# Both expert matmuls by Strassen's seven products

## The chip, the cores and the metric

The kernel runs on one core of a Trainium2 chip. A core has a matmul engine (PE), three engines for elementwise work (DVE, ACT, POOL), a queue for transfers (SP) and 16 DMA engines between DRAM and its own memory (SBUF; matmuls write to a second memory, PSUM, of eight banks). The metric is the device time of one execution in microseconds (us); lower is better. The kernel before took 2241.37 us in the median of three runs, 2239.83 to 2242.37.

## The reference, cut to what matters

Two layers. The first is attention with decay: for each of 4 sequences and 8 heads a 64 x 64 state is decayed by gamma and a product k v is added at each of 768 positions, and q reads it. The second takes the 3072 x 512 result as x:

```
P = exp(x @ w_gate - max); 8 times: rows, then columns of P are normalized
out = 0
for e in range(8):                          # experts
    h = max(x @ w1[e], 0)                   # 3072 x 512 times 512 x 1024
    out += P[:, e:e+1] * (h @ w2[e])        # 3072 x 1024 times 1024 x 512
```

Every token goes through all eight experts.

## The kernel before

**Precision.** The two expert matmuls run in a reduced format of fp32 that PE takes at full rate. To keep accuracy each operand is split into a high part (a copy, rounded) and a low part (the operand minus its high part), and each product is three matmuls: high x high, low x high, high x low. ACT or POOL makes high parts (`hi_act`, L72, or a cast, L112), DVE or POOL the low ones (`lo`, L75).

**Attention.** 24 chunks of 128 positions (6 chunks of each of 4 sequences). `split_qk` splits q and k, `scores` (L226) multiplies them into `ps_s`, DVE masks the result into `ta` (L229), `attend` (L257, L262) reads the state and adds the chunk's own part, `state` (L238, L244) updates the state. Beside it the kernel already runs the first expert group in units of 256 tokens, and the gate logits.

**Experts.** The hidden dimension of all experts, 8 x 1024, is cut into 16 groups of four tiles of 128. For a group g and a block i of 512 tokens, `b_mm1` makes one hidden tile in `hps2` by 12 matmuls of 512 columns (`mm1`, L121 to L123), `h_split` (L126 on ACT, L127 on DVE) makes the high and low half of its relu, and one tile later `b_mm2` multiplies it with w2 into four banks `ops2` (`mm2`, L132 to L134). After four tiles DVE adds the four banks, times the gate value, to the accumulators `acc` in SBUF (L460 for the first group, L462 then), and the last group stores them (L465). Accumulators of all 3072 tokens stay in SBUF. `x_split` splits the next block's x while this one is multiplied (L72, L75), and POOL splits the weights of the next group (`conv_w`). The 18 steps of the gate normalization are strewn between the first tiles.

Everything stands in the order in which it is written (`manual_schedule`): each engine runs its instructions in that order, and waits by semaphores.

## Time and profile before

| | |
|---|---|
| median of three runs | 2241.37 us |
| the profiled execution's span, first to last instruction | 2238.8 us |
| PE matmul busy | 2219.1 us, 99% |
| PE weight loads busy | 1856.5 us, 83% |
| DVE, ACT, POOL busy | 892.5, 523.2, 349.4 us |
| DMA | 87.46 MB, mean 39 GB/s |
| matmul and weight-load instructions | 10639 each |

Times are of one execution, taken by the hardware profiler. A group's row reads: line, engine, operation, output <- inputs, shapes, count | busy us, mean ns of one | idle time of the engine ahead of it, and what ended it. In rows ordered by time the first number is the start in us from the span's start and the second the length. Matmuls overlap their successors, so one that lasts 0.39 us does not occupy PE for so long; the interval between starts does. The granted clock is the share of full speed that the throttle gives PE.

### The profile page before, as it was taken

To read this page: it belongs to the slowest core of one execution; us is meant where nothing else is said; L and a number is where in the kernel's file an instruction comes from. 1 tells how busy PE (TensorE), PEld (TensorE's weight loads), DVE (VectorE), ACT (ScalarE), POOL (GpSimd) and SP (SyncE) were. 2 spreads that over 40 slices of the span, in tenths; PEclk is the share of its full clock that TensorE was granted. 3 is DMA by queue.
4 is the path that set the end of the run, shared out by engine and by line. 5 is a ranking of instruction groups with operands and counts; after the bars stand their busy time and mean duration, and the time that the engine had idled before them with its cause. 6 is when DMAs were issued, how large, how long until landed. Compare 5 with 4: busy or idle time off the path is not lost.

```text
span 2238.8 us, 25404 instructions
## 1 busy us (share of the span) xinstructions
PE 2219.1 (99%) x10639; PEld 1856.5 (83%) x10639; DVE 892.5 (40%) x1403; ACT 523.2 (23%) x949; POOL 349.4 (16%) x329
## 2 busy tenths in 40 slices
PE   7999999999999999999999999999999999999999
PEld 6999888888888888888888888888888888888887
DVE  5666455333433333343333334333333433333342
ACT  4333321332212122121222212122221212222121
POOL 5554200202020020202002020200202020020200
PEclk9999999999999999999999999999999999999999
DMA  6454350101010010101001010100101010010011
GB/s 206 132 169 128 125 172 5 33 1 38 1 33 6 6 34 1 38 1 33 5 5 34 1 38 1 34 5 5 33 1 38 1 34 5 6 33 1 10 57 57
DMA packets 91027, 87.46 MB, mean 39 GB/s; under 512 B 5792, under 2 KB 66336, under 8 KB 90912
## 3 DMA queue, kind: packets, MB, share of 16 engines
q1 hardware_dynamic: 90624, 84.78, 12.1%
q8 instruction: 84, 1.38, 0.3%
q0 software_dynamic: 288, 1.05, 0.2%
q14 instruction: 31, 0.25, 0.0%
HBM read 69.03 MB, written 16.78 MB: 38 GB/s over the span
## 4 chain that ended last, share of the span: by engine, by line
PE 98%; DVE 1%; SPq 0%; ACT 0%; DMA 0%; issue 0%; ACTq 0%
PE hps L121 16%; PE ops L133 16%; PE ops L132 16%; PE ops L134 16%; PE hps L123 15%; PE hps L122 15%; PE ps_s L226 1%; PE ps_x L262 1%; PE ps_t L238 1%; PE ps_x L257 1%; DVE QL L75 1%; DMA raw<-qT 0%; SPq L176 0%; PE ps_g L291 0%; PE ps_g L290 0%
## 5 line engine op out<-in xcount | busy, mean ns | idle before, releaser
L127 DVE SCALAR_TENSOR_TENSOR hl<-hps,hh 128x512 fp32r<-128x512 f32 x360 | 249.0, 692 | 1218.3 <-ACT hh L126 1218.3
L126 ACT ACTIVATE hh<-hps 128x512 fp32r<-128x512 f32 x360 | 215.6, 599 | 1540.8 <-PE hps L123 1535.4
L123 PE MATMUL hps<-xl,w1h 128*128 128x512 f32 x1440 | 560.6, 389 | 0.9 <-DVE xl L75 0.9
L121 PE MATMUL hps<-xh,w1h 128*128 128x512 f32 x1440 | 561.4, 390 | 0.0
L133 PE MATMUL ops<-w2l,hh 128*128 128x512 f32 x1440 | 560.3, 389 | 0.0
L122 PE MATMUL hps<-xh,w1l 128*128 128x512 f32 x1440 | 560.3, 389 | 0.0
L134 PE MATMUL ops<-w2h,hl 128*128 128x512 f32 x1440 | 560.2, 389 | 0.0
L132 PE MATMUL ops<-w2h,hh 128*128 128x512 f32 x1440 | 560.2, 389 | 0.0
L123 PEld LDWEIGHTS hps<-xl,w1h 128*128 128x128 f32 x1440 | 270.2, 188 | 57.8 <-DVE xl L75 1.4
L121 PEld LDWEIGHTS hps<-xh,w1h 128*128 128x128 f32 x1440 | 270.6, 188 | 56.2
L133 PEld LDWEIGHTS ops<-w2l,hh 128*128 128x128 f32 x1440 | 270.4, 188 | 56.4
L134 PEld LDWEIGHTS ops<-w2h,hl 128*128 128x128 f32 x1440 | 270.4, 188 | 56.0
L132 PEld LDWEIGHTS ops<-w2h,hh 128*128 128x128 f32 x1440 | 270.0, 188 | 55.9
L122 PEld LDWEIGHTS hps<-xh,w1l 128*128 128x128 f32 x1440 | 270.2, 188 | 55.6
L112 POOL CAST w1h<-r 128x512 fp32r<-128x512 f32 x55 | 33.6, 611 | 1450.4 <-PE hps L123 1450.4
L75 DVE TENSOR_TENSOR xl<-x,xh 128x512 fp32r<-128x512 f32 x360 | 229.7, 701 | 0.0
L462 DVE SCALAR_TENSOR_TENSOR acc<-ops,Pm,acc 128x512 f32<-128x512 f32 x336 | 228.4, 743 | 2.1 <-PE ops L134 2.1
L72 ACT ACTIVATE xh<-x 128x512 fp32r<-128x512 f32 x360 | 196.6, 622 | 0.0
L75 POOL TENSOR_TENSOR w1l<-r,w1h 128x512 fp32r<-128x512 f32 x63 | 82.3, 1307 | 43.7 <-ACT w1h L72 36.8
L75 POOL TENSOR_TENSOR w2l<-r,w2h 128x512 fp32r<-128x512 f32 x63 | 86.5, 1373 | 4.4
L75 DVE TENSOR_TENSOR QL<-raw,QH 64x512 fp32r<-64x512 f32 x46 | 61.4, 1334 | 14.6 <-ACT QH L72 13.9
L112 POOL CAST w2h<-r 128x512 fp32r<-128x512 f32 x55 | 36.8, 670 | 141.7 <-PE ops L134 141.7
(101 smaller groups left out, 1163.4 us busy)
## 6 DMA issues: line engine op xcount, KB each, us to landing
r<-w SPq DMA_DIRECT2D x128, 256.0 KB, 2.7
raw<-kT SPq DMA_DIRECT2D x24, 256.0 KB, 4.1
raw<-qT SPq DMA_DIRECT2D x24, 256.0 KB, 3.6
raw<-vn SPq DMA_DIRECT2D x24, 256.0 KB, 5.2
spill<-y SPq DMA_DIRECT2D x24, 256.0 KB, 2.0
acc<-spill SPq DMA_DIRECT2D x24, 256.0 KB, 6.4
out<-acc SPq DMA_DIRECT2D x24, 256.0 KB, 2.1
raw<-kn SPq DMA_DIRECT2D x20, 256.0 KB, 5.2
```

What stands on the lines that cost most here:

```text
L72: act.activation(o, i, AF.Copy)
L75: eng.tensor_tensor(o, full, rd(h), ALU.subtract)
L112: engs[0].tensor_copy(h, r)
L121: pe.matmul(hps[:, :n], w[0][:, k, :], xh[:, k, :], start=(k == 0), stop=False)
L122: pe.matmul(hps[:, :n], w[1][:, k, :], xh[:, k, :], start=False, stop=False)
L123: pe.matmul(hps[:, :n], w[0][:, k, :], xl[:, k, :], start=False, stop=(k == KD - 1))
L126: act.activation(hh, hps[:, :n], AF.Relu)
L127: dve.scalar_tensor_tensor(hl, hps[:, :n], 0.0, rd(hh), ALU.max, ALU.subtract)
L132: pe.matmul(ops[t], hh[:, s], w[2], start=(f == 0), stop=False)
L133: pe.matmul(ops[t], hh[:, s], w[3], start=False, stop=False)
L134: pe.matmul(ops[t], hl[:, s], w[2], start=False, stop=(f == FG - 1))
L462: dve.scalar_tensor_tensor(acc[m], o, Pm[:, m, e:e + 1], acc[m], ALU.mult, ALU.add)
```

## The change

x, w1, h and w2 are cut into 2 x 2 blocks of 256 x 256 (a stretch of 512 hidden units, a chunk of 4 x 128 tokens), and each 2 x 2 block product is formed by seven products of sums and differences of blocks (Winograd's form of Strassen's algorithm, M1 to M7) in place of eight. Each of the seven is still three high/low matmuls over two halves of the contraction and two of the output: 12 matmuls of 256 columns.

The work now stands in two stages. In the first, each of 96 units (16 stretches of hidden units x 6 chunks, `a_step`) multiplies sums of x with sums of w1. PE accumulates in four banks; ACT and DVE combine the seven products (`a_post`), take the relu, and form the four blocks of h and the four sums of them that the second stage needs, seven slices of 128 x 512 in all, that go to DRAM (`hd`). In the second stage a block is one expert and one chunk: two stretches (`jl`) of seven products, 14 steps. SP loads a slice of h for each step 14 steps ahead (`h_load`), ACT and DVE make its high and low part three steps ahead (`h_conv`), and PE multiplies it with sums of w2 (`b_mm`), both stretches into the same seven banks. In the second stretch `b_post` combines the products, scales the result with the gate values (L744, four copies on ACT), and the sum goes to DRAM: plainly for the first expert, by an adding transfer that POOL issues for the other seven. The accumulators in SBUF are gone.

Sums of w1 and w2 are formed and split by POOL (high parts by ACT), those of x by DVE or DVE and POOL, a task at a time between PE's steps (`conv_tasks`, `run`). Beside attention only the stretch 0 of the hidden units runs now. The gate logits are made with plain fp32 matmuls of 8 columns, and the normalization's 18 steps stand between units 2 to 19 of the first stage.

```diff
-UNIT = 256
-NU = N // UNIT
-BLK = 512
-NBLK = N // BLK
+BLK = B * C
 NTILE = N // P
-FG = 4
-NG = E * F // (FG * P)
+HB = BLK // 2
+NJP = E * F // 512
...
+ORD_U = [M1, M5, M2, M6, M3, M7, M4]
+ORD_W1 = [M1, M2, M5, M6, M3, M7, M4]
+ORD_B = [M1, M2, M6, M7, M5, M3, M4]
...
-    def mm1(hps, w, xh, xl, n):
-        for k in range(KD):
-            pe.matmul(hps[:, :n], w[0][:, k, :], xh[:, k, :], start=(k == 0), stop=False)
-            pe.matmul(hps[:, :n], w[1][:, k, :], xh[:, k, :], start=False, stop=False)
-            pe.matmul(hps[:, :n], w[0][:, k, :], xl[:, k, :], start=False, stop=(k == KD - 1))
-
-    def h_split(hps, hh, hl, n):
-        act.activation(hh, hps[:, :n], AF.Relu)
-        dve.scalar_tensor_tensor(hl, hps[:, :n], 0.0, rd(hh), ALU.max, ALU.subtract)
-
-    def mm2(ops, w, hh, hl, f, nt):
-        for t in range(nt):
-            s = slice(t * P, (t + 1) * P)
-            pe.matmul(ops[t], hh[:, s], w[2], start=(f == 0), stop=False)
-            pe.matmul(ops[t], hh[:, s], w[3], start=False, stop=False)
-            pe.matmul(ops[t], hl[:, s], w[2], start=False, stop=(f == FG - 1))
-
...
+    NSA, NSB = 16, 17
+    SLA = cst.tile([P, NSA, 2, 2, HB], F32R, name="SLA")
+    RAW = [cst.tile([P, 4, 512], F32, name=f"RAW{i}") for i in range(3)]
+    SC = cst.tile([P, 4, 512], F32, name="SC")
+    OUTS = cst.tile([P, 8, 512], F32, name="OUTS")
+    TMP = cst.tile([P, 6, 512], F32, name="TMP")
+
+    xd = [drp.tile([P, 4, 512], F32, name=f"xd{i}") for i in range(CPB)]
+    hd = [[drp.tile([P, 7, 512], F32, name=f"hd{j}_{i}") for i in range(CPB)] for j in range(NJP)]
+
...
+    def sums_left(b, s):
+        a11, a12, a21, a22 = b
+        s1, s2, s3, s4 = s
+        return ([(s1, a21, a22, ALU.add), (s2, s1, a11, ALU.subtract),
+                 (s3, a11, a21, ALU.subtract), (s4, a12, s2, ALU.subtract)],
+                [a11, a12, s4, a22, s1, s2, s3], {M5: [0], M6: [0, 1], M7: [2], M3: [0, 1, 3]})
+
+    def sums_right(b, t, neg3):
+        b11, b12, b21, b22 = b
+        t1, t2, t3, t4 = t
+        x, y = (b12, b22) if neg3 else (b22, b12)
+        return ([(t1, b12, b11, ALU.subtract), (t2, b22, t1, ALU.subtract),
+                 (t3, x, y, ALU.subtract), (t4, b21, t2, ALU.subtract)],
+                [b11, b21, b22, t4, t1, t2, t3], {M5: [0], M6: [0, 1], M7: [2], M4: [0, 1, 3]})
+
...
+    def conv_tasks(sums, slots, order, eng_add, eng_lo, done=None):
+        adds, src, need = sums
+        engs = eng_lo if isinstance(eng_lo, list) else [eng_lo] * 7
+        tasks, made = [], set()
+
+        def add(a):
+            eng_add.tensor_tensor(a[0], a[1], a[2], a[3])
+
+        def one(i, e):
+            t = slot(slots[i])
+            hi_act(t[:, 0], src[i])
+            lo(e, t[:, 1], src[i], t[:, 0])
+
+        for k, i in enumerate(order):
+            for a in need.get(i, ()):
+                if a not in made:
+                    made.add(a)
+                    tasks.append((k, lambda a=adds[a]: add(a)))
+            tasks.append((k, lambda i=i, e=engs[k]: one(i, e)))
...
+    def a_mm(u, i):
+        bank = {M1: "A", M6: "A", M7: "A", M4: "A", M2: "B", M5: "C", M3: "C"}[i]
+        new = i in (M1, M2, M5)
+        if new:
+            u.t[bank] = psA[bank]()
+        ps = u.t[bank]
+        w, x = slot(u.w[i]), slot(u.x[i])
+        for j in range(2):
+            for k in range(2):
+                for n, (a, b) in enumerate(((0, 0), (1, 0), (0, 1))):
+                    pe.matmul(ps[:, j, :], w[:, a, k, j * P:(j + 1) * P], x[:, b, k, :],
+                              start=new and j == 0 and k == 0 and n == 0,
+                              stop=j == 1 and k == 1 and n == 2, **kw)
+
...
+    def a_post(u, i):
+        t = u.t
+        if i == M1:
+            t["s1"] = TMP[:, 0, :]
+            act.activation(t["s1"], flat(t["A"]), AF.Copy)
+        elif i == M5:
+            t["s5"] = TMP[:, 1, :]
+            act.activation(t["s5"], flat(t["C"]), AF.Copy)
+        elif i == M2:
+            o = a_out(u, "A11")
+            dve.tensor_tensor(o, flat(t["B"]), t["s1"], ALU.add)
+            act.activation(o, o, AF.Relu)
+            a_store(u, "A11", M1)
+        elif i == M6:
+            t["u2"] = TMP[:, 2, :]
+            act.activation(t["u2"], flat(t["A"]), AF.Copy)
+        elif i == M3:
+            t["c12"] = TMP[:, 3, :]
+            dve.tensor_tensor(t["c12"], flat(t["C"]), t["u2"], ALU.add)
+            o = a_out(u, "S3")
+            dve.scalar_tensor_tensor(o, t["c12"], 0.0, t["A11"], ALU.max, ALU.subtract)
+            a_store(u, "S3", M7)
+        elif i == M7:
+            o = a_out(u, "A22")
+            dve.tensor_tensor(o, flat(t["A"]), t["s5"], ALU.add)
+            act.activation(o, o, AF.Relu)
+            a_store(u, "A22", M4)
+            s1 = a_out(u, "S1")
+            dve.scalar_tensor_tensor(s1, t["c12"], 0.0, o, ALU.max, ALU.add)
+            a_store(u, "S1", M5)
+            s2 = a_out(u, "S2")
+            dve.tensor_tensor(s2, s1, t["A11"], ALU.subtract)
+            a_store(u, "S2", M6)
+        elif i == M4:
+            o = a_out(u, "A12")
+            act.activation(o, flat(t["A"]), AF.Relu)
+            a_store(u, "A12", M2)
+            s4 = a_out(u, "S4")
+            dve.tensor_tensor(s4, o, t["S2"], ALU.subtract)
+            a_store(u, "S4", M3)
+
...
+        sweep = [[5, 4, 3], [0, 1, 2]]
+        units = [(0, 0, 5)] + [(s, jp, c) for s in range(2) for jp in range(1, NJP) for c in sweep[s]]
...
+            seq = [(u, M6), (v, M1), (u, M3), (u, M7), (v, M2), (u, M4), (v, M5)]
+            for m, (w, i) in enumerate(seq):
+                if w is not None:
+                    a_step(w, i)
+                if n > 0 or m > 0:
+                    run(bg, 2)
+                if m % 2 == 0:
+                    run(wq, 1)
+                if job == NJP - 1 and row < 2 and m == 5:
+                    bg += x_conv(sweep[1][row])
+            if 2 <= n < 2 + len(sink):
+                sink[n - 2]()
+            if row == 2:
+                run(wq, 12)
...
+        HR = XS[0] + XS[2]
+        corder = [5, 4, 3, 0, 1, 2]
+        steps = [(e, c, jl, i) for e in range(E) for c in corder for jl in range(2) for i in ORD_B]
...
+        def w2_conv(e, jl):
+            r = raw_at.pop(("w2", e, jl))
+            sl = {i: w2_slot(e, 7 * jl + k) for k, i in enumerate(ORD_B)}
+            t = conv_tasks(sums_right(blocks_w2(r), scratch(SC), True), sl, ORD_B, pool, pool, lambda: raw_done(r))
+            last = NW2 - 14
+            return [(SPE * e + (14 - SPE if k + 7 * jl < last else k + 7 * jl - last - 14), f) for k, f in t]
+
+        def h_load(s):
+            if s < len(steps):
+                e, c, jl, i = steps[s]
+                sp.dma_start(rd(slot(HR[s % NH])[:, 1]).rearrange("p j t -> p (j t)"), hd[2 * e + jl][c][:, i, :])
+
+        def h_conv(s):
+            if s < len(steps):
+                t = slot(HR[s % NH])
+                act.activation(t[:, 0], rd(t[:, 1]), AF.Copy)
+                lo(dve, t[:, 1], rd(t[:, 1]), t[:, 0])
...
+            ps = cur[i]
+            h = slot(HR[s % NH])
+            w = slot(w2_slot(e, 7 * jl + ORD_B.index(i)))
+            for j in range(2):
+                for t in range(2):
+                    for n, (a, b) in enumerate(((0, 0), (0, 1), (1, 0))):
+                        pe.matmul(ps[:, t, :], h[:, a, j, t * P:(t + 1) * P], w[:, b, j, :],
+                                  start=jl == 0 and j == 0 and t == 0 and n == 0,
+                                  stop=jl == 1 and j == 1 and n == 2, **kw)
...
+            if i == M2:
+                dve.tensor_tensor(cc[:, 0, :, 0, :], cur3, h3(m1s), ALU.add)
+            elif i == M6:
+                dve.tensor_tensor(U2, ps, m1s, ALU.add)
+            elif i == M7:
+                dve.tensor_tensor(uu[:, 1, :], ps, U2, ALU.add)
+            elif i == M5:
+                act.activation(m5s, ps, AF.Copy)
+            elif i == M3:
+                dve.tensor_tensor(uu[:, 0, :], ps, U2, ALU.add)
+            elif i == M4:
+                dve.tensor_tensor(cc[:, 1, :, 0, :], cur3, h3(uu[:, 1, :]), ALU.add)
+                for r in range(2):
+                    dve.tensor_tensor(cc[:, r, :, 1, :], h3(uu[:, r, :]), h3(m5s), ALU.add)
+                c4 = pt["cc"]
+                for b in range(4):
+                    act.activation(c4[:, b, :], c4[:, b, :], AF.Copy, scale=Pm[:, B * c + b, e:e + 1])
+                o = out.rearrange("(b s) d -> s b d", b=B)[c * C:(c + 1) * C]
+                if e == 0:
+                    sp.dma_start(o, c4)
+                else:
+                    pool.dma_start(o, c4, accum_op=ALU.add)
...
+        for s in range(len(steps)):
+            e, c, jl, i = steps[s]
+            b_mm(s)
+            b_post(s)
+            h_conv(s + 3)
+            h_load(s + NH)
+            for _ in range(2 if s < 14 else 1):
+                if pend and pend[0][0] <= s:
+                    run(pend, 1)
+            r = s % SPE
+            if e + 1 < E:
+                if r == 14:
+                    w2_load(e + 1, 0)
+                    w2_load(e + 1, 1)
+                if r == 20:
+                    pend += w2_conv(e + 1, 0)
+                    pend += w2_conv(e + 1, 1)
```

`hi_act`, `lo`, attention and the normalization's arithmetic are unchanged.

552 lines of the change are left out of this document (286 added, 266 removed).

## The prediction

> **What bounds the kernel now.** I read the page first, for its busy times and its chain of waits.
>
> ```profile
> span 2238.8 us, 25404 instructions
> PE 2219.1 (99%) x10639; PEld 1856.5 (83%) x10639; DVE 892.5 (40%) x1403; ACT 523.2 (23%) x949; POOL 349.4 (16%) x329
> PE 98%; DVE 1%; SPq 0%; ACT 0%; DMA 0%; issue 0%; ACTq 0%
> ```
>
> The chain that ends last is PE for 98%. A busy PE could still wait between its matmuls, so next come two stretches, the attention stage's steady part and the expert stage (columns: us, then busy time of PE, weight load, DVE, ACT, POOL, granted clock, DMA share, GB/s), and four starts of matmuls: the first and the last of 24 with 256 columns, and of 12 with 512.
>
> ```profile
> 60.00:222.00 162.00, 162.00 (x1304) 148.83 (x1303) 106.51 (x160) 60.33 (x118) 86.27 (x64) 1.00 0.47 145
> 390.00:2160.00 1770.00, 1770.00 (x7810) 1465.62 (x7810) 641.33 (x978) 380.44 (x678) 212.61 (x218) 1.00 0.06 17
> 104.16 0.28 PE L121 MATMUL hps<-uxh,w1h 128*128 128x256 f32 x1
> 106.77 0.28 PE L226 MATMUL ps_s<-QH,kl 128*128 128x256 f32 x1
> 1002.74 0.39 PE L121 MATMUL hps<-xh,w1h 128*128 128x512 f32 x1
> 1005.23 0.39 PE L123 MATMUL hps<-xl,w1h 128*128 128x512 f32 x1
> ```
>
> A matmul starts every 1770/7810 = 0.2266 us at 512 columns, and every 2.61/23 = 0.1135 us at 256: half the columns cost half the time, although each brings its own weight load. So PE's matmul stream is the kernel, and other engines have 60% and more to spare.
>
> **What PE is spared.** Experts took 16 groups x 6 blocks x 96 = 9216 matmuls of 512 columns, 2088 us. Strassen leaves 7 of 8: 2 stages x 96 units x 7 products x 12 = 16128 of 256 columns, at 0.1134 us 1829 us. A product's twelve are a step of 1.36 us, a unit 9.52 us, and a block of the second stage (14 steps) 19.04 us. The gift is 259 us. Everything else is what the other engines now do between the products.
>
> **The end of a block of the second stage.** This is where I look first, because only three steps of h are converted ahead. Prices (four scaled copies and four additions in a row; groups with their mean ns):
>
> ```profile
> 415.28 2.55 ACT L544 ACTIVATE acc<-acc,Pm 128x512 f32<-128x512 f32 x4
> 299.57 2.48 DVE L460 TENSOR_TENSOR acc<-ops,acc 128x512 f32<-128x512 f32 x4
> L72 ACT ACTIVATE xh<-x 128x512 fp32r<-128x512 f32 x360 | 196.6, 622 | 0.0
> L75 DVE TENSOR_TENSOR xl<-x,xh 128x512 fp32r<-128x512 f32 x360 | 229.7, 701 | 0.0
> L276 ACT ACTIVATE xu<-ps_x 128x512 f32<-128x512 f32 x16 | 9.6, 599 | 69.4 <-PE ps_x L262 69.4
> acc<-spill SPq DMA_DIRECT2D x24, 256.0 KB, 6.4
> ```
>
> ACT in the kernel before: one evacuation for each hidden tile, and the next x far ahead of its use.
>
> ```order
> L126 ACTIVATE hh<-hps_5430 128x512 [waits DVE_49,PE_49]
> L72 ACTIVATE xh<-x_3300 128x512 x4
> L126 ACTIVATE hh<-hps_5473 128x512 [waits DVE_49,PE_49]
> L126 ACTIVATE hh<-hps_5502 128x512 [waits DVE_49,PE_49]
> L126 ACTIVATE hh<-hps_5531 128x512 [waits DVE_49,PE_49]
> ```
>
> ACT in the change, around the last product (M4) of a block; L691 makes the high half of an h slice, L735 evacuates M5, L744 scales the output:
>
> ```order
> L735 ACTIVATE TMP<-psM_12565 128x512 [waits PE_49,Activation_49]
> L691 ACTIVATE SLA<-SLA 128x512 [waits DMAHW0_49,Activation_49]
> L691 ACTIVATE SLA<-SLA 128x512 [waits DMAHW1_49,Activation_49]
> L744 ACTIVATE OUTS<-OUTS,Pm 128x512 [waits DMASW0_49,DVE_49]
> L744 ACTIVATE OUTS<-OUTS,Pm 128x512
> L744 ACTIVATE OUTS<-OUTS,Pm 128x512 [waits DVE_49]
> L744 ACTIVATE OUTS<-OUTS,Pm 128x512
> L691 ACTIVATE SLA<-SLA 128x512 [waits DMAHW2_49,Activation_49]
> ```
>
> The third L691 moved behind four copies that wait for M4; DVE stands alike, with M4's three additions ahead of that slice's low half:
>
> ```order
> L737 TENSOR_TENSOR TMP<-psM_12565,TMP 128x512 [waits PE_49]
> L76 TENSOR_TENSOR SLA<-SLA 128x512 [waits DMAHW1_49,Activation_49]
> L739 TENSOR_TENSOR OUTS<-psM_12566,TMP 128x2x256 [waits DVE_49,PE_49]
> L741 TENSOR_TENSOR OUTS<-TMP 128x2x256 [waits DVE_49]
> L741 TENSOR_TENSOR OUTS<-TMP 128x2x256
> L76 TENSOR_TENSOR SLA<-SLA 128x512 [waits DMAHW2_49,Activation_49]
> ```
>
> What moved: evacuating a block now precedes the conversion that PE needs two steps later. Both engines take 0.70 us for one such operation and start the next 0.61 us later ((2.55 - 0.71)/3). I count from the block's start. M5 is seen ended at 16.5; its copy and the two high halves behind it end at 17.1, 17.6 and 18.2, so DVE starts the low half of step 14 at 17.7, M3's addition at 18.3, the low half of step 15 at 18.9 and L739 at 19.5, when M4 (end 19.04, seen at 19.2, since a matmul lasts 0.28 us at a start interval of 0.11) is long there. The first L741 ends at 20.85. ACT scales from 20.9 and is free 4 x 0.61 later, at 23.35; the high half ends at 23.95, the low half at 24.7. PE's third matmul of step 16 needs it, so that step starts at 24.5; its cover, steps 14 and 15, ended at 21.76. **PE waits 2.7 us after every block**: 47 x 2.75 = 129 us (110 to 150 with 0.3 us either way), and behind PE's wait the rest of that block is simply later. Inside a block nothing is late: M1's and M5's copies, 0.6 + 0.62 + 0.70 = 1.9 us, lie under 2.7. SP queues each h load behind the step that frees its slot, 11 steps (15 us) before its conversion, against 6.4 us to landing.
>
> **What the wait does to the clock.** Stretches of 3.41 us, in pairs (low PE, then its successor), and one near the end:
>
> ```profile
> 17.79:21.21 3.42, 1.44 (x10) 1.23 (x10) 2.49 (x5) 3.36 (x7) 1.64 (x1) 1.00 1.04 320
> 21.21:24.62 3.41, 3.41 (x19) 3.41 (x18) 3.35 (x4) 0.88 (x2) 3.41 (x3) 0.50 0.89 254
> 34.86:38.27 3.41, 1.25 (x10) 1.15 (x10) 2.86 (x4) 1.50 (x4) 3.01 (x3) 1.00 0.17 51
> 38.27:41.69 3.42, 3.42 (x14) 2.38 (x14) 1.13 (x2) 0.00 (x0) 3.18 (x3) 0.50 0.70 215
> 48.51:51.93 3.42, 1.68 (x14) 1.47 (x13) 3.06 (x5) 0.52 (x2) 3.42 (x3) 1.00 0.00 1
> 51.93:55.34 3.41, 3.41 (x12) 2.83 (x11) 1.94 (x3) 0.00 (x0) 0.06 (x1) 0.50 0.00 0
> 2233.02:2236.44 3.42, 2.04 (x9) 1.34 (x8) 2.79 (x4) 0.00 (x0) 0.00 (x0) 1.00 0.53 195
> ```
>
> PE busy for 1.25 to 1.68 us of such a stretch got half the clock in the next; 2.04 us did not cost it. So about 1.8 us of idle time inside one stretch is enough. A wait of 2.7 us at a random place puts that much into one stretch with chance (1.6 + 0.9)/3.41 = 0.75, and half a stretch is then lost, 1.7 us; the longer waits below always do it. 47 x 0.8 x 1.7 = 64 us (0 to 80).
>
> The Trainium skill, "TensorE: Matmul & The Clock Gate", Part 1, has the clock fall only after a whole idle window of about 3.4 us. By that rule 2.7 us cost nothing here and the sum below would be 64 us lower; the three pairs differ from it, and I go by them.
>
> **POOL beside DVE.** Two DVE subtractions alone and beside POOL, with POOL's rows of that time:
>
> ```profile
> 18.11 1.39 DVE L75 TENSOR_TENSOR QL<-raw,QH 64x512 fp32r<-64x512 f32 x2
> 91.63 2.81 DVE L75 TENSOR_TENSOR QL<-raw,QH 64x512 fp32r<-64x512 f32 x2 [0.35 <-ACT QH L72]
> 91.16 1.29 POOL L75 TENSOR_TENSOR kl<-raw,kh 128x512 fp32r<-128x512 f32 x1 [1.81 <-ACT kh L72]
> 92.40 1.49 POOL L205 TENSOR_TENSOR tk<-raw,gk 128x512 f32<-128x512 f32 x1
> 93.86 1.75 POOL L198 TENSOR_TENSOR tq<-raw,gq 128x512 f32<-128x512 f32 x1
> ```
>
> Beside POOL arithmetic a DVE operation with two SBUF inputs doubles. In the second stage POOL converts the next expert's w2 (22 operations) in the second and the last block of each expert. There the low halves and both L741 take up to 1.4 us, DVE falls behind from M2 on, and the wait after M4 grows by some 3 us: 14 x 3 = 42 us (0 to 80).
>
> **First stage.** DVE, before four L462 after each block, has seven dependent operations in a unit:
>
> ```order
> L222 TENSOR_TENSOR TMP<-psC,TMP 128x512 [waits PE_49,Activation_49]
> L224 SCALAR_TENSOR_TENSOR OUTS<-TMP,OUTS 128x512 [waits DMAHW0_49,DVE_49]
> L228 TENSOR_TENSOR OUTS<-psA_183,TMP 128x512 [waits DMAHW1_49,PE_49]
> L232 SCALAR_TENSOR_TENSOR OUTS<-TMP,OUTS 128x512 [waits DMAHW2_49,Activation_49]
> L235 TENSOR_TENSOR OUTS<-OUTS 128x512 [waits DMAHW3_49,DVE_49]
> L214 TENSOR_TENSOR OUTS<-psB,TMP 128x512 [waits DMAHW4_49,PE_49]
> ```
>
> What moved in: from M3's end, L222, L224 and L228 follow, ACT's relu, L232, L235, L214, and two relus more before the bank is free that the next unit's M1 writes: six DVE operations 0.62 to 0.73 us apart and three or four ACT operations 0.6 apart make 6.2 to 6.8 us, and PE's own way from M3 to that M1 is five steps, 6.8. Just covered; with L224 doubled by POOL (w1 conversions fill about half the time) some 0.45 us are not. 90 units x 0.45 = 40 us (0 to 144, if L232 and L235 double too).
>
> **Attention stage, the turns and the end.**
>
> ```profile
> 22.04 2.56 PE ps_s L226 x12
> 105.69 1.36 PE ps_s L226 x12
> 126.78 1.36 PE ps_s L226 x12
> L75 DVE TENSOR_TENSOR QL<-raw,QH 64x512 fp32r<-64x512 f32 x46 | 61.4, 1334 | 14.6 <-ACT QH L72 13.9
> L229 DVE TENSOR_TENSOR ta<-ps_s,msk 128x512 f32<-128x512 f32 x48 | 31.4, 686 | 8.0 <-DMA msk<-c_msk 5.1 <-PE ps_s L226 2.7
> L244 DVE TENSOR_TENSOR st<-ps_t,st 64x256 f32<-64x256 f32 x32 | 13.3, 416 | 0.2
> L75 POOL TENSOR_TENSOR w1l<-r,w1h 128x512 fp32r<-128x512 f32 x63 | 82.3, 1307 | 43.7 <-ACT w1h L72 36.8 <-DMA ident<-c_id 2.5
> 300.00:308.00 8.00, 8.00 (x38) 6.63 (x37) 7.31 (x17) 3.20 (x6) 0.00 (x0) 1.00 1.07 373
> 2233.84 2.37 SPq L465 DMA_DIRECT2D out<-acc  x4
> ```
>
> Two chunks took 21.09 us with PE full. A chunk now holds less PE work, and DVE sets it: 2 x 1.33, 2 x 0.69, 2 x 0.42, a quarter of 11 x-conversions at 0.7 to 1.4 (2.9) and of a unit's seven (1.2), 9.0, taken as 9.3 with waits. 22 (start of chunk 2) + 22 x 9.3 = 227, and 20 for converting the last x and, on POOL, the second w1 (9 x 1.3 = 12 us): 247 us (230 to 280), six units being done. Gate normalization and five more x conversions: 15 us (0 to 30). Turn to the second stage: last stores, w2 and h loads queued behind them, then POOL's 22 conversions at 1.3 to 1.75 against 19 us of PE: 26 us (15 to 40). End: 2.1 + 2.5 us of evacuation and a megabyte's store of 2.4 us or, accumulating, some three times that: 12 us (8 to 20).
>
> DMA: h goes out at 1.84 MB plus 0.35 MB of w1 a unit, 229 GB/s, and comes in at 3.67 + 0.35 MB a block, 10.8 us at the 373 GB/s of 300 to 308 us; 1.05 MB of accumulating output is 2.8 us as a plain move, and no row shows it accumulating. Taken as two passes, 5.6, the block's 22 us hide it all.
>
> **Sum**: 247 + 90 x 9.52 = 857 + 40 + 15 + 26 + 48 x 19.04 = 914 + 129 + 64 + 42 + 12 = 2346 us against the span of 2238.8; the median runs shown, 2241.4, lie 2.6 above it: **2349 us, 4.8% slower**. The 259 us saved on matmuls go into waits that the kernel before has not.
>
> **Rivals.** (1) Cover is better than I think: the 2.7 us stand, but neither clock nor POOL follows them, and DVE is not the attention stage's limit: 2349 - 64 - 42 - 40 - 15 - 15 = 2173 us, **faster**. For it: 2.7 us is near the edge of the clock's condition, and POOL idles in four blocks of six. Against: the three pairs, and 1.39 against 2.81. It decides where those terms come out under 110 us together. (2) The accumulating stores decide: from 11 us of all engines each (four passes) a block exceeds its 22 us; at eight passes 42 blocks take 10.8 + 22.4 = 33 us, about 2349 + 42 x 9 = 2730. Against: adding would have to cost four times a plain move. POOL's w2 conversions queue behind these stores, which wait for ACT's L744, but those are due some eighteen steps after their slots come free. (3) 256-column matmuls keep an interval seen in the attention stage, (100.80 - 99.86)/8 = 0.1175 us, instead of 0.1135:
>
> ```profile
> 99.86 0.28 PE L121 MATMUL hps<-uxh,w1h 128*128 128x256 f32 x1
> 100.80 0.28 PE L123 MATMUL hps<-uxl,w1h 128*128 128x256 f32 x1
> ```
>
> That is 16128 x 0.0041 = 66 us more, 2415. For it: weight loads are busy 83% already. Against: 0.1135 was seen beside the same loads, and both stages are free of the fp32 attention matmuls.
>
> **Chances**: forecast 0.62 (2270 to 2440 us), rival 1 0.20, rival 2 0.08, rival 3 0.07, no difference 0.03. A difference under 0.2% could not be told. Faster 0.19, same 0.03, slower 0.78; the range 2180 to 2470 reaches into rivals 1 and 3.
>
> **What would show it.** In the second stage PE idle after each block's M4, ended by DVE's low half behind ACT's L744, near 2.7 us, and half-clock stretches behind it; longer in the second and last block of an expert; start intervals of 0.1135; 10 us a unit in the first stage with M1 waiting for ACT. No gap at the blocks' ends would make it wrong at its root, and landings of L749 beyond 20 us would speak for rival 2.

## The result and the profile after

The changed kernel takes **2568.81 us** in the median of four runs (2565.83 to 2570.00); the kernel before, beside it, 2241.57. The ratio is 1.146, with a 95% interval of 1.1446 to 1.1478. The forecast of slower holds, but its 2349 us lie 220 us too low, and the range (2180 to 2470) did not hold the time.

The page of the changed kernel, its span, busy times and chain of waits:

```profile
span 2568.1 us, 46250 instructions
PE 2258.2 (88%) x17335; PEld 2195.4 (85%) x17335; DVE 1531.5 (60%) x2008; ACT 1136.6 (44%) x2044; POOL 913.3 (36%) x660
PE 58%; DVE 14%; issue 11%; ACT 6%; DMA 5%; POOL 4%; SPq 0%; DVEq 0%; ACTq 0%; POOLq 0%
```

PE was 98% of the chain before and is 58% now; DVE, ACT and POOL have come into it. Cut by stage (attention with the first six units; the other 90 units; the turn; the 48 blocks; the end; columns as in the prediction):

```profile
0.00:324.80 324.80, 238.84 (x1692) 222.37 (x1693) 193.04 (x249) 112.30 (x197) 138.47 (x110) 0.82 0.43 134
324.80:1310.40 985.60, 937.83 (x7579) 924.35 (x7579) 571.37 (x751) 431.94 (x774) 458.85 (x333) 0.98 0.56 203
1310.40:1334.70 24.30, 0.33 (x4) 0.13 (x2) 1.41 (x3) 5.28 (x10) 12.90 (x11) 0.55 0.82 291
1334.70:2553.80 1219.10, 1081.19 (x8064) 1048.56 (x8064) 763.81 (x1005) 584.47 (x1060) 301.76 (x207) 0.92 0.75 195
2553.80:2568.10 14.30, 0.00 (x0) 0.00 (x0) 1.89 (x3) 2.56 (x4) 1.28 (x1) 0.67 0.46 73
```

The second row could not be read from such a table alone, since a busy PE hides how densely its matmuls start. So I read the starts of two steps of the first stage that follow each other, twelve matmuls in a row each:

```profile
642.15 1.60 PE L188 MATMUL psA<-SLB,SLA 128*128 128x256 f32 x12
643.59 1.60 PE L188 MATMUL psA<-SLB 128*128 128x256 f32 x12
```

A step takes 1.44 us, not 1.36: a matmul of 256 columns starts every **0.1200 us**, where the prediction had 0.1134. What PE waited for, over the whole run (us, times, longest):

```profile
PE psM L708 <- ACT SLA L691: 125.7, 48, 24.0
PE psA L188 <- DVE OUTS L228: 66.7, 42, 6.6
...
PE psM L708 <- DVE SLA L76: 27.2, 54, 2.4
```

The first row is the turn (24.0) and one wait a block; the third comes right behind it; the second is that of the units. Set against the sum of the prediction:

| part | predicted | measured | difference |
|---|---|---|---|
| attention and six units | 247 | 324.8 | +78 |
| matmuls of 90 units (7560) | 857 | 907.2 | +50 |
| what stands between them (stalls, normalization, x) | 40 + 15 | 985.6 - 907.2 = 78.4 | +23 |
| turn | 26 | 24.3 | -2 |
| matmuls of 48 blocks (8064) | 914 | 967.7 | +54 |
| waits, clock and POOL in the blocks | 129 + 64 + 42 = 235 | 1219.1 - 967.7 = 251.4 | +16 |
| end | 12 | 14.3 | +2 |
| sum | 2346 | 2568.1 | +222 |

Two terms carry the miss: the start interval (+104) and the attention stage (+78). Waits, clock and POOL in the blocks, on which the prediction spent most words, came out within 7%.

The end of a block stands in the chain as it was foretold. A piece of the chain of waits around the M4 of one block (start, length, what), the changed kernel:

```profile
1440.58 0.69 DVE OUTS L739
1441.27 0.61 DVE OUTS L741
...
1441.90 0.63 ACT OUTS L744
...
1443.14 1.32 ACT OUTS L744 x2
1444.46 0.53 ACT SLA L691
...
1445.01 0.70 DVE SLA L76
...
1445.76 2.40 PE psM L708 x10
```

L739 and L741 on DVE, four L744 on ACT, then the high half (L691) and the low half (L76) of the slice that PE needs, and only then PE.

### The profile page after: what moved, and what is told of

Same layout as the page of the kernel before. It is cut to its first block, busy times and chain, and to the rows that moved or that the text cites. A ratio compares the mean times of both kernels' runs of the same rounds, so it can differ in the third digit from the quotient of the medians.

```text
span 2568.1 us, 46250 instructions
## 1 busy us (share of the span) xinstructions
PE 2258.2 (88%) x17335; PEld 2195.4 (85%) x17335; DVE 1531.5 (60%) x2008; ACT 1136.6 (44%) x2044; POOL 913.3 (36%) x660
## 4 chain that ended last, share of the span: by engine, by line
PE 58%; DVE 14%; issue 11%; ACT 6%; DMA 5%; POOL 4%; SPq 0%; DVEq 0%; ACTq 0%; POOLq 0%
PE psM L708 25%; PE psA L188 17%; PE psC L188 9%; DVE SLA L76 3%; ACT OUTS L744 2%; DMA SLB<-hd 2%; DMA RAW<-w 2%; PE psB L188 2%; POOL SC L137 2%; DVE TMP L222 2%; DVE OUTS L228 2%; DVE QL L76 2%; PE ps_s L353 2%; ACT SLA L691 1%; PE ps_x L386 1%
## 5 line engine op out<-in xcount | busy, mean ns | idle before, releaser
L76 DVE TENSOR_TENSOR SLB<-SLB 128x512 fp32r<-128x512 f32 x336 | 278.2, 851 | 273.5 <-ACT SLB L691 273.2
L76 DVE TENSOR_TENSOR SLA<-SLA 128x512 fp32r<-128x512 f32 x336 | 298.3, 928 | 200.0 <-ACT SLA L691 199.2
L708 PE MATMUL psM<-SLB,SLA 128*128 128x256 f32 x2016 | 316.7, 318 | 98.8 <-ACT SLA L691 78.1
L708 PEld LDWEIGHTS psM<-SLB,SLA 128*128 128x128 f32 x2016 | 293.4, 223 | 117.5 <-ACT SLA L691 85.4
L708 PE MATMUL psM<-SLA 128*128 128x256 f32 x2016 | 289.4, 304 | 54.4 <-ACT SLA L691 47.5
L708 PEld LDWEIGHTS psM<-SLA 128*128 128x128 f32 x2016 | 276.2, 212 | 63.1 <-ACT SLA L691 50.0
L188 PE MATMUL psA<-SLB,SLA 128*128 128x256 f32 x2136 | 293.2, 288 | 25.9 <-DVE OUTS L228 24.8
L188 PEld LDWEIGHTS psA<-SLB,SLA 128*128 128x128 f32 x2136 | 271.0, 194 | 35.0 <-DVE OUTS L228 34.2
L708 PE MATMUL psM<-SLB 128*128 128x256 f32 x2232 | 283.3, 285 | 6.6 <-DVE SLB L76 3.3
L708 PEld LDWEIGHTS psM<-SLB 128*128 128x128 f32 x2232 | 274.5, 193 | 10.1 <-DVE SLB L76 6.6
L76 POOL TENSOR_TENSOR SLA<-SC,SLA 128x512 fp32r<-128x512 f32 x120 | 162.3, 1362 | 235.7 <-ACT SLA L73 159.2
L76 POOL TENSOR_TENSOR SLA<-RAW,SLA 128x512 fp32r<-128x512 f32 x93 | 124.8, 1344 | 330.5 <-ACT SLA L73 330.1
L691 ACT ACTIVATE SLA<-SLA 128x512 fp32r<-128x512 f32 x336 | 188.9, 616 | 0.0
L691 ACT ACTIVATE SLB<-SLB 128x512 fp32r<-128x512 f32 x336 | 187.8, 618 | 0.0
L744 ACT ACTIVATE OUTS<-OUTS,Pm 128x512 f32<-128x512 f32 x192 | 122.9, 710 | 141.0 <-DVE OUTS L741 141.0
```

Source lines behind the costliest of these rows:

```text
L76: eng.tensor_tensor(o, full, rd(h), ALU.subtract)
L188: pe.matmul(ps[:, j, :], w[:, a, k, j * P:(j + 1) * P], x[:, b, k, :], start=new and j == 0 and k == 0 and n == 0, stop=j == 1 and k == 1 ...
L691: act.activation(t[:, 0], rd(t[:, 1]), AF.Copy)
L708: pe.matmul(ps[:, t, :], h[:, a, j, t * P:(t + 1) * P], w[:, b, j, :], start=jl == 0 and j == 0 and t == 0 and n == 0, stop=jl == 1 and j ...
L744: act.activation(c4[:, b, :], c4[:, b, :], AF.Copy, scale=Pm[:, B * c + b, e:e + 1])
```

## The experiments

A time that stands without a ratio is that of a single execution.

### The block's end: six steps of lead

Theory: the wait is the conversion that stands behind M4's evacuation. Rivals: POOL beside DVE keeps DVE late whatever the lead; or a bank is missed in its place.

```diff
+        for s in range(3, 6):
+            h_conv(s)
...
-            h_conv(s + 3)
+            h_conv(s + 6)
```

> h slices are converted six steps ahead in place of three; nothing else is changed. My theory, the wait after each block's M4 is the conversion queued behind the scaled copies and takes the clock down with it: the 154 us that PE waits for L691 and L76 of SLA and some 97 us of half clock go, the second stage falls from 1219 us to 1020 to 1060, the kernel to 2370 to 2410 (ratio to the kernel before 1.06 to 1.075). Rival, POOL's w2 conversions slow DVE so much in two blocks of six that it is behind whatever the lead: only the four other blocks gain, 3.3 us each, 2568 - 110 = 2460. Rival, the lead makes M4's evacuation later and a bank is missed instead: no gain, 2550 or more.

Measured: 2409.60 us, ratio 1.0758 (1.074 to 1.0776). The second stage of e2_ahead6 in one row:

```profile
1328.70:2386.90 1058.20, 1002.55 (x8064) 988.46 (x8064) 756.26 (x1005) 584.31 (x1060) 300.17 (x207) 0.98 0.83 225
```

161 us are gone from it, and the granted clock rises from 0.92 to 0.98. Four blocks of six now take exactly 20.16 us, fourteen steps of 1.44, so nothing at all is left of the wait there, although all adding stores of the output run as before. The other two take 29.4 (after an expert's last block) and 22.9 us (after its second), in the median: the same two blocks in six that were long before, 28.4 and 29.0 against 22.7 to 25.4. The theory is right for four blocks of six, and the first rival for the one after an expert's last; the one after its second gained 6 us.

### POOL beside DVE: one w2 for all experts

```diff
-            return W2R[(14 * e + k) % NW2]
+            return W2R[k % NW2]
...
-            if e + 1 < E:
+            if e < 0:
                 if r == 14:
```

> w2 of expert 0 is converted once and used for all experts; w2 loads and POOL's conversions (22 operations an expert) are left out for experts 1 to 7. My theory, POOL's SBUF operations double DVE's in two blocks of six: the long blocks (28.4 and 28.8 us on average, against 24.1 and 22.7 for the others) fall to 24, the second stage by 14 x 4.5 = 63 us to about 1156. Rival, the long blocks come from something else (POOL's adding stores, loads of w2 on the DMA queues ahead of h): they stay at 28 us if it is the adding stores; if it is loads of w2 they would fall as well, but the DVE operations' length would not.

Measured: 2507.61 us. Second stage of e4_no_w2, and the low halves on DVE in one stretch of it (count, then shortest, median and longest in ns):

```profile
1335.40:2491.50 1156.10, 1065.49 (x8064) 1041.36 (x8064) 627.43 (x1005) 530.42 (x962) 70.21 (x53) 0.92 0.76 193
L76 DVE TENSOR_TENSOR SLA<-SLA x289: 679/684/693, 1413.6 to 2395.6; 128x512 fp32r<-128x512 f32 x145
```

The same operations in the changed kernel:

```profile
L76 DVE TENSOR_TENSOR SLA<-SLA x276: 676/687/3603, 1398.6 to 2389.6; 128x512 fp32r<-128x512 f32 x138
```

The second stage is 63.0 us shorter, as expected, and every block from the seventh on takes 23.9 us. Without POOL no low half lasts over 0.693 us; beside it the longest takes 3.603. The Trainium skill, "SBUF — State Buffer", "SBUF: two separate sides", says that DVE with two SBUF inputs and a GpSimd operation that reads SBUF take a shared port pair by an exclusive lock. This pair of rows agrees in that DVE's operations lengthen; the lock itself is not seen in it. This run left out the loads of w2 too, so it prices both together; the split came later, in e6 and e7.

### The clock: filling the wait

In e4 every block is alike, so one more edit can be read from it: 14 matmuls without use ahead of the third step of a block, where PE waits.

```diff
+            if s % 14 == 2 and s > 14:
+                ...
+                for n in range(14):
+                    pe.matmul(ps[:, 0, :], h1[:, 0, 0, 0:P], w1_[:, 0, 0, :], start=n == 0, stop=n == 13, **kw)
```

> e4_no_w2 (one expert's w2 for all, three steps ahead), and into the wait after each block's M4, ahead of the third step of the next block, PE gets 14 matmuls more of 256 columns (1.7 us) into that step's bank, which the step then overwrites. In e4_no_w2 every such block takes 23.89 us: 14 x 1.44 = 20.16, a wait of about 2.2, and 1.5 that I put down to half clock. My theory, the clock falls because PE is idle for 1.8 us or more in one stretch of 3.41: with the hole filled it stays at 1.00, and a block takes 22.2 to 22.6 us although PE does more work; the kernel 2507 - 48 x 1.5 = 2435. Rival, the half clock has another cause (what follows M4, the block's rhythm) or the 1.5 us are work that is late in itself: the block stays at 23.89 us or grows.

Measured: 2445.01 us, 62.6 us less than e4 with 658 matmuls more. The second stage of e5_fill:

```profile
1333.40:2429.20 1095.80, 1077.63 (x8722) 1057.03 (x8722) 627.62 (x1005) 530.84 (x962) 70.24 (x53) 0.99 0.77 204
```

The granted clock goes from 0.92 to 0.99, and a block from 23.89 to 22.65 us. So the block's 3.73 us over 20.16 were 2.49 of wait and 1.24 of half clock. The prediction had 2.75 and 64/47 = 1.36. By the rule of the Trainium skill that was weighed there (a whole idle window), 2.49 us would have cost nothing more; this run decides for the traces' three pairs. Two neighbouring stretches of e4_no_w2 show such a fall:

```profile
2015.13:2018.54 3.41, 1.66 (x14) 1.46 (x13) 0.87 (x3) 3.30 (x6) 0.45 (x1) 1.00 0.67 183
2018.54:2021.96 3.42, 3.36 (x15) 3.07 (x16) 3.42 (x6) 3.42 (x7) 0.83 (x1) 0.50 0.76 109
```

PE is busy for 1.66 us of the first, and the second has half the clock. In e4 this returns in every block: the blocks start 23.89 us apart, which is seven stretches of 3.413, so each meets them alike. The 1.24 us are the price at this length; for blocks of another length e5 does not tell it.

### The start interval: forms of matmuls

First the forms that tell why 256 columns take 0.1200 us here:

```diff
+            if e == 6:          # six matmuls of 512 columns
+                ...pe.matmul(flat(ps), h[:, a, j, 0:P], w[:, b, :, :].rearrange("p j d -> p (j d)"), ...
+                        if e == 2:      # two of 128 columns
+                        elif e == 4:    # two of 64 weight columns
+                if e == 5:      # no loads of h
+                    return
```

> Only PE's matmuls of the second stage are changed, and only in some experts, so that the interval between starts can be read for each form: expert 2, each matmul cut into two of 128 columns (same sums); expert 4, each done as two with 64 weight columns (half of the outputs are left out); expert 5, as it is, but without its loads of h (stale h); expert 6, six matmuls of 512 columns a step in place of twelve of 256 (wrong sums); experts 0, 1, 3, 7 as they are. Measured before it: 0.120 us at 256 columns everywhere in the changed kernel, 0.2266 at 512 and 0.1134 at 256 in the kernel before. Theory 1, PE takes an instruction only every 0.06 us, so a weight load and a matmul cost at least 0.120: expert 2 0.120 a matmul (a step of 2.88 us), expert 4 0.120, expert 5 0.120, expert 6 0.2266. Theory 2, loading 128 weight columns takes 0.120: expert 2 0.120, expert 4 about 0.1134, expert 5 0.120, expert 6 0.2266. Theory 3, every column costs 0.120/256 in this kernel: expert 2 about 0.06 (a step stays 1.44 us), expert 4 0.120, expert 6 0.240. Theory 4, transfers into SBUF slow PE's reads: expert 5 alone goes to 0.1134. The regular hole of 0.99 us in 252 matmuls should come once in so many instructions under an instruction-fetch theory: in expert 2 per 252 matmuls of half the size, in expert 6 hidden or half as often.

Expert 4 (64 weight columns, an early and a later stretch), expert 6 (512 moving columns) and expert 2 (128 moving columns: its first step, then two later) of e1_forms:

```profile
2240.89 2.96 PE L723 MATMUL psM<-SLB,SLA 128*64 128x256 f32 x24
2243.68 6.58 PE L723 MATMUL psM<-SLB 128*64 128x256 f32 x55
...
2321.88 16.48 PE L723 MATMUL psM<-SLB 128*64 128x256 f32 x144
...
2626.72 5.60 PE L710 MATMUL psM<-SLA,SLB 128*128 128x512 f32 x24
2632.16 2.88 PE L710 MATMUL psM<-SLB,SLA 128*128 128x512 f32 x12
...
1641.17 5.53 PE L719 MATMUL psM<-SLB,SLA 128*128 128x128 f32 x48
1654.82 15.56 PE L719 MATMUL psM<-SLA 128*128 128x128 f32 x72
1670.18 5.32 PE L719 MATMUL psM<-SLB,SLA 128*128 128x128 f32 x24
```

Starts: with 64 weight columns first 2.79/24 = 0.116 us, later (16.48 - 0.28)/143 = 0.113, where 0.28 is the length of the last matmul; with 512 columns 5.44/24 = 0.2267. With 128 columns the first step runs at (5.53 - 0.28)/47 = 0.112, then (from 1654.82) at 15.36/72 = 0.2133. Expert 5, without its h loads, stays at 0.120 (median of its 1007 intervals), so the loads of h are not the cause. An instruction limit of 0.06 us (theory 1) falls with 0.116 and 0.112; 0.120 on every load (theory 2) falls with 0.112; a share on every column (theory 3) falls with 0.2267 in place of 0.240. None of the four was right as it stood. The regular hole of 0.99 us in 252 matmuls, which I had put to instruction fetch, is a wait for L228 in the trace and belongs to the first stage (below).

A second table of forms, one in each expert:

```diff
+            cfg = {1: (32, 256), 2: (96, 256), 3: (128, 192), 5: (128, 320), 6: (128, 384)}.get(e)
...
+            if e == 4:
+                order.sort(key=lambda x: x[1])    # output halves in turn
```

> Again only the forms of PE's matmuls in the second stage, one by expert, twelve a step (values of these experts are not the reference's, parts of the products are left out or wrong): expert 1, 32 weight columns by 256 moving ones; expert 2, 96 by 256; expert 3, 128 by 192; expert 4, 128 by 256 as it is, but the two output halves in turn instead of one after the other; expert 5, 128 by 320; expert 6, 128 by 384; experts 0 and 7 as they are. From e1_forms: 128 by 256 0.120, 64 by 256 0.1146, 128 by 512 0.227 us. My theory, the load of 128 weight columns (about 0.107 us) is just hidden no more behind 256 columns (0.1134): 32 by 256 0.1134, 96 by 256 between 0.1146 and 0.120, 128 by 192 0.108 to 0.118 (not 0.085), 128 by 320 0.1417 to 0.148, 128 by 384 0.170, and expert 4 stays 0.120. Rival, successive additions to the same PSUM columns cost the 0.0066: expert 4 alone goes to 0.1134, and 32 by 256 stays at 0.1146 or more. Rival, a share of 18/16 on every column: 320 takes 0.150 and 384 0.180.

Rows of e8_forms2, in the order 32 weight columns (a pair of neighbours, then one from the next block), 192 moving columns, halves in turn, 320, 384 (pairs of neighbours):

```profile
1500.66 4.40 PE L721 MATMUL psM<-SLA 128*32 128x256 f32 x36
1504.90 4.40 PE L721 MATMUL psM<-SLA,SLB 128*32 128x256 f32 x36
...
1524.38 4.24 PE L721 MATMUL psM<-SLA 128*32 128x256 f32 x36
...
1808.57 4.18 PE L721 MATMUL psM<-SLA,SLB 128*128 128x192 f32 x36
1812.59 4.18 PE L721 MATMUL psM<-SLB 128*128 128x192 f32 x36
...
1961.91 8.80 PE L721 MATMUL psM<-SLB 128*128 128x256 f32 x72
1970.55 1.60 PE L721 MATMUL psM<-SLA,SLB 128*128 128x256 f32 x12
...
2113.66 7.20 PE L711 MATMUL psM<-SLA,SLB 128*128 128x320 f32 x48
2120.70 5.44 PE L711 MATMUL psM<-SLB 128*128 128x320 f32 x36
...
2279.58 6.40 PE L711 MATMUL psM<-SLB 128*128 128x384 f32 x36
2285.82 8.48 PE L711 MATMUL psM<-SLA,SLB 128*128 128x384 f32 x48
```

| moving columns | weight columns | starts every, us | columns/2400 us | rest |
|---|---|---|---|---|
| 512 | 128 | 0.2267 | 0.2133 | 0.0133 |
| 384 | 128 | 6.24/36 = 0.1733 | 0.1600 | 0.0133 |
| 320 | 128 | 7.04/48 = 0.1467 | 0.1333 | 0.0133 |
| 256 | 128 | 0.1200 | 0.1067 | 0.0133 |
| 256, halves in turn | 128 | 8.64/72 = 0.1200 | 0.1067 | 0.0133 |
| 256 | 96 | 0.1161 (mean at full clock) | 0.1067 | 0.0094 |
| 256 | 64 | 0.116 or 0.113 | 0.1067 | 0.010 or 0.007 |
| 256 | 32 | 4.24/36 = 0.1178, or (4.24 - 0.28)/35 = 0.113 | 0.1067 | 0.011 or 0.006 |
| 192 | 128 | 4.02/36 = 0.1117 | 0.0800 | 0.0317 |
| 128 | 128 | 0.112 | 0.0533 | 0.058 |

With 128 weight columns it is a straight line from 256 columns up: (0.2267 - 0.1200)/256 = 1/2400 us for a column **and 0.0133 us for each matmul**. Below that a floor of 0.11 us takes over, where only the weight load of 128 columns was left alike. The PSUM rival and the rival of 18/16 on every column fall; mine held for the floor and for 320, and nearly for 384 (0.1733 for 0.170). For narrow weights it held in part: 32 and 64 weight columns run at 0.113 in some blocks and at 0.116 to 0.118 in others, while of the some 880 intervals of an expert with 128 weight columns at full clock fewer than five lie under 0.116. So the width of the weight load has a share in the rest. What else it is made of, and what chooses between the two values, stays open.

The kernel before shows both values too, with 128 weight columns. Of the 490 intervals at full clock between neighbouring matmuls of its first expert group (256 columns, L121 to L123) 221 are 0.112 to 0.115 us, those of the prediction among them, and 269 are 0.116 or more; the median is 0.117. Why stays open as well.

### The attention stage

Left out beside the attention: five units and the conversions of x for them (the second stage reads the next stretch's h in their place).

```diff
             def unit_steps(c):
+                if c < CPB - 1:
+                    return
```

> Leaves out, beside the attention, the five units of hidden stretch 0 (chunks 0 to 4) and the conversions of x for them; the second stage reads stretch 1 twice in their place. Theory A, the DVE, ACT and PE steps of the attention form a chain of their own that takes 12.8 us a chunk: the last attention matmul stays at 270 to 290 us. Theory B, the attention waits because DVE does the units' sums and the conversions of x, in program order, between its own operations: 9 us a chunk or less without them, the last attention matmul at 180 to 230 us. The rest of the kernel unchanged in both.

Measured: 2508.97 us. Then the same with q and k split earlier in program order:

```diff
+                if tau > 3:
+                    split_qk(tau + 2)
                 attend(tau)
-                if tau > 3:
-                    split_qk(tau + 2)
```

> e3_bare_attention with one edit more: q and k of chunk tau+2 are split ahead of attend(tau) in program order, no longer behind it, so that ACT does not reach them only after the evacuation of attend's result. In e3 the last attention matmul stood at 234 us, 9.6 us a chunk. My theory, the chain from attend through ACT's evacuation, kh, QH and DVE's QL to the next scores sets that pace: the last attention matmul comes to 200 to 220 us. Rival, engines' own work (DVE, POOL beside it) sets it: 230 us or more, and what e6_combined gained in the attention (27 us) came from its other edits.

Measured: 2450.49 us. The last attention product's group of rows (count, durations in ns, first and last start) of the changed kernel, of e3 and of e9:

```profile
L386 PE MATMUL ps_x<-ta,raw x384: 272/273/477, 8.7 to 284.5; 128*64 128x128 f32 x192
```

```profile
L386 PE MATMUL ps_x<-ta,raw x384: 272/273/477, 9.2 to 234.3; 128*64 128x128 f32 x192
```

```profile
L386 PE MATMUL ps_x<-ta,raw x384: 272/273/477, 9.1 to 172.4; 128*64 128x128 f32 x192
```

From 22 us on, a chunk takes 11.9 us, 9.7 without the units and 6.8 with the split moved. The first run's 234.3 us lie between its two theories, the second's 172.4 below what was expected. The five units cost 50 us beside the attention and would cost 5 x 10.1 after it: nothing of them was hidden. And the attention without them was paced by the order of its own instructions, which the one moved call shows. The chain of the changed kernel has the same order (from 100 us on):

```profile
100.41 1.05 PE ps_x L386 x16
...
101.48 0.02 ACT RAW L391
...
101.97 0.62 ACT kh L73
102.59 0.53 ACT QH L73
...
103.14 0.69 DVE QL L76
...
104.54 1.43 DVE QL L76
...
108.96 1.29 DVE SLA L76 x2
...
110.28 0.70 DVE TMP L222
...
112.36 2.93 PE psA L188 x12
```

attend's result (L386) is evacuated on ACT (L391); only behind that stand kh and QH of a later chunk; DVE makes QL, then x's and the unit's sums; then PE may go on to the unit and to the next attend. The prediction counted how long each engine is busy; here each step waits for another engine's.

### Putting the repairs together

> Correct and complete, five edits that can be read apart by stage. Second stage: h converted six steps ahead as in e2_ahead6, h slots 14 to 12 and w2 slots 19 to 21, so that the first stretch's w2 is converted one task every four steps and the second's over 18 steps in place of 9. First stage: L224 (S3) behind L228, which PE waits for, and x converted one task a step in place of two in the last two jobs. Attention: q and k split ahead of attend in place of behind. My theory, each of these stalls is what the trace names: second stage from 1219 us to 985 to 1010 (all blocks near 20.16), first stage's 0.33 us a unit gone (30 us) and the stall at 805 to 870 us (26 us) at least halved, attention shorter by 0 to 40 us: kernel 2210 to 2290. Rival, POOL's conversions cost DVE the same wherever they stand: blocks with them stay near 23 and 29 us, and the kernel at 2330 to 2360. With 0.1200 us a matmul, 16128 matmuls alone are 1935 us, so that it comes to within 2% of the kernel before at best.

The edits, beside those shown: S3 (L224) behind L228; 12 slots for h and 21 for w2; the tasks of w2 at their own times.

```diff
-            last = NW2 - 14
-            return [(SPE * e + (14 - SPE if k + 7 * jl < last else k + 7 * jl - last - 14), f) for k, f in t]
+            if jl == 0:
+                return [(SPE * e + 20 - SPE + 4 * n, f) for n, (k, f) in enumerate(t)]
+            return [(SPE * e - 14 + max(k, int(1.5 * n)), f) for n, (k, f) in enumerate(t)]
```

Measured: 2344.98 us, ratio 1.0458 (1.0441 to 1.0476), outside the 2210 to 2290 expected; part of x is converted behind its use there. Read by stage: the first stage's 0.33 us a unit are gone, its undisturbed units take 10.08 = 7 x 1.44 (L224, slowed by POOL, had held up L228, and PE waits for that one). The attention with six units ended 27 us earlier. The second stage gained nothing against e2: its long blocks are 25.5 and 26.7 us. The rival looked right, until the blocks after an expert's second (26.7 us) were looked up: in the 48 us around such a block POOL did six operations, but 2 MB of w2 stood ahead of the h loads on SP.

> Complete and in the right order again (e6_combined took x too late in the last jobs: there its conversions stand behind their use). Kept from e6: six steps ahead, 12 h slots and 21 w2 slots, L224 behind L228, q and k split ahead of attend. New: w2 goes in as 256 KB pieces, one every second step, where 2 MB stood ahead of the h loads on SP; the sums for the second stretch's w2 are made ahead, so that 7 of 11 POOL operations are left in an expert's last block; w2 of expert 0 is loaded and converted during the last units of the first stage. My theory, in e6 the long blocks after an expert's second (26.7 us) come from h loads that stand behind w2's 2 MB, and those after its last (25.5 us) from POOL beside DVE; the turn of 25 us is the loading and converting of w2 behind the last stores. Then the first kind falls to 20.2, the second to 22 to 24, the turn to 5 us or less: 2343 - 7 x 6.5 - 7 x 2.5 - 20 + 5 (x in two tasks a step again) = 2265 (2245 to 2290). Rival, the first kind is POOL beside DVE too: it stays at 25 or more and the kernel at 2300 or more.

The loads of w2, in pieces:

```diff
+                for q in range(4):
+                    lq.append(lambda q=q: sp.dma_start(
+                        r[:, q, :], w2[e, jl * 512 + q * P:jl * 512 + q * P + P, :]))
...
+            if r % 2 == 0 and lq:
+                lq.pop(0)()
```

Measured: 2309.85 us, ratio 1.0301 (1.0284 to 1.0318). The second stage takes 1033.7 us, at a granted clock of 0.99. The long blocks come to 22 to 24 us, both kinds, and the turn to 8 us in place of 24. That the blocks after an expert's second fall with the loads in pieces fits my theory, though they fall to 21.8 to 24.0 and not to 20.2; the start of their conversions moved too, so it isn't shown by that alone. But the blocks that had been at 20.2 to 20.5 us in e6 now stand at 21.5, and the kernel is 20 us above the range that was expected. Tasks 3.5 in place of 4 steps apart, pieces of w2 beside h: which of them does it was not taken apart.

> e7_combined2, complete, with the units of hidden stretch 0 taken out of the attention: only chunk 4's stands at its end, those of the other five chunks come as a job between the two sweeps of the first stage, with w1 of that stretch loaded and split a second time; x of chunks 0 to 3 is no longer converted beside the attention, and x of the second sweep is converted one task a step over a longer time. In e7 six units were done at 299 us; in e9_bare_split the bare attention ended at 172. My theory, the units beside the attention cost more there than the 10.1 us they take later: six units would be done at about 172 + 60 to 75 = 232 to 247 us if they stood in a row, so 50 to 65 us are won there, and 10 to 25 us from the x conversions (68 us for four units in e7): kernel 2225 to 2260. Rival, the attention hides the units' matmuls after all and e9's gain was the missing work alone: 2300 or more.

```diff
-        units = [(0, 0, 5)] + [(s, jp, c) for s in range(2) for jp in range(1, NJP) for c in sweep[s]]
+        units = [(0, 0, 4)] + [(0, jp, c) for jp in range(1, NJP) for c in sweep[0]]
+        units += [(2, 0, c) for c in (5, 3, 0, 1, 2)] + [(1, jp, c) for jp in range(1, NJP) for c in sweep[1]]
```

Measured: 2260.52 us, ratio 1.0082 (1.0066 to 1.0099): 49 us from taking the units out of the attention and giving x more time. It lands at the upper edge of what was expected. Last, the lead, `h_conv(s + 7)` and then `h_conv(s + 8)`:

> e10_units_after with h converted seven steps ahead in place of six, 12 slots as before, so that a load of h has 5 steps (7.2 us) to land. In e10, 29 of the 47 block intervals are 21.5 to 22.1 us, 1.4 us above 14 steps of 1.44. My theory, those 1.4 us are the low halves that DVE makes late beside POOL, and a step more of lead (1.44 us) is enough for them: those blocks come to 20.2, the second stage from 1030 to about 990 us, the kernel from 2260 to 2220 to 2232, under the kernel before (ratio 0.990 to 0.996). Rival, the lateness adds up over a block, so that a lead is used up once and won back never: 21.5 stays and the kernel at 2250 or more.

> The same with eight steps of lead, so that a load has 4 steps (5.8 us) against a median of about 4.3 to landing. My theory, it gains a few us more where seven steps do not cover the blocks of 22 to 24 us: 2212 to 2230. Rival, loads of h now land late where w2's pieces stand ahead of them, and PE waits for L716 behind DMA: 2235 or more, slower than seven.

Measured: 2240.53 us, ratio 0.9995 (0.9986 to 1.0004), and 2240.19 us, ratio 0.9992 (0.9982 to 1.0002). Seven steps win 20 us: of the five blocks in six that took 21.5 or more, two come to 20.16 and three stay near 21.5. The second stage takes 1014.1 us, so 990 us was too good, the kernel misses its 2220 to 2232, and the rival has a part. With eight, ACT waits longer for the loads of h (for the slices in SLB 104.3 us in 61 waits, against 73.4 in 64), as that run's rival had it, but the kernel is not slower for it: the two leads end alike. Neither can be told from the kernel before. All repairs together give back 328 us and reach the start; no version here beats it.

## Why the prediction was wrong, and where it was right

**The start interval: wrong step, about half of the miss.** "Half the columns cost half the time" was read from 24 starts at 0.1134 us, and taken for a price of columns. At full clock and with 128 weight columns it is columns/2400 plus 0.0133 us a matmul in every form from 256 to 512 columns, in a long run. Strassen's cut to 256 columns doubles the number of matmuls and so that fixed part: 9216 x 0.0133 = 123 us before, 16128 x 0.0133 = 215 us after. The gift is 2088 - 1935 = 153 us, not 259. Rival 3 had the right row (0.1175) and the right kind, "an interval seen in the attention stage", but at 66 us for 106 and with a chance of 0.07; a price that the whole sum rests on deserved more than one short stretch, and the trace of the kernel before had more such intervals at 0.116 and above (269) than at 0.113 (221). The Trainium skill, "TensorE: Matmul & The Clock Gate", "Back-to-back issue gap", has for an isolated matmul columns/2.4 + 2.5 ns at full clock and columns/1.2 at half: 0.2133 at half clock agrees with it, 0.1200 at full does not (it would be 0.1092).

**The attention stage: wrong step, 78 us.** "A chunk now holds less PE work, and DVE sets it: 9.0, taken as 9.3" added up busy times of one engine. DVE was busy for 193 of 324.8 us. The chunk was paced by a chain over ACT, DVE and PE in program order, 11.9 us. For the attention without the units e9 shows it by one moved call (9.7 to 6.8 us), and e3 shows that the units were not hidden at all; in the whole kernel the same move, with L224 behind L228, brought 27 us (e6), and taking the units out, with more time for x, another 49 (e10). Of the 78 us, 22 x (11.9 - 9.3) = 57 lie in the chunks; 20 more lie behind the last one, where 324.8 - 284.5 = 40 us stand for the 20 of the prediction.

**The wait after M4: right, 2.75 predicted, 2.49 measured** (e5), in the place and through the instructions foretold, and gone with more lead (e2). **The clock: right**, 1.36 and 1.24 us a block (e5). **POOL beside DVE: the place and the mechanism right**, two blocks of six, 42 us predicted and 63 measured with what the clock adds (e4, which prices w2's loads together with it; e6 and e7 speak for a part of those, which the prediction did not have). By these prices 47 x 2.49 + 47 x 1.24 + 63 = 238 of the 251.4 us; most of the other 13 lie in the first block, which takes 31.5 us in e4. The starts in the changed kernel itself say the same another way: 716 of its intervals between the blocks' matmuls are 0.205 to 0.222 us in place of 0.120, which is half clock and costs 67 us (64 predicted; 40 falls, 47 x 0.8 = 38 predicted), and the other 184 us stand in longer intervals, the waits (129 + 42 = 171).

**The first stage: right mechanism, a little larger.** L224 beside POOL costs PE 0.33 us on average in an undisturbed unit (they take 10.08 to 10.75), for 0.45 predicted; the x conversions for the second sweep and the start cost 49 us, for 15 (the stall near 805 us alone is 26).

**Turn and end**: 24.3 for 26, 14.3 for 12. That an accumulating store takes "some three times" a plain one had no row behind it; on the page of the changed kernel a megabyte lands in a median of 9.4 us accumulating (42 stores) and 5.2 plain (6). **Rival 2** (adding stores) falls: blocks of 20.16 us in e2 hold them. **Rival 1** (better cover, 2173) falls: every wait it would have dropped was there.

## What to carry to other kernels

Cutting a matmul into smaller ones saves streaming, not matmuls: price it by an interval measured over a long run of the very form, here, with 128 weight columns, columns/2400 us plus 0.0133 each, with a floor near 0.11. Busy shares do not tell whether work fits beside a stage; follow one item through the engines in program order, and ask which instruction stands ahead of the one that is waited for. Where a wait returns in every block, it can cost more than itself: here 2.49 us cost another 1.24 in clock, and lead, or even useless matmuls in the wait, took that away.
